# A recurrence fused with a feed-forward layer: shared table loads, one step's row sums on VectorE, another load order and new queue orders

## The chip, the cores and the metric

The kernel runs on one core of a Trainium2 chip. The metric is the device time of one execution in microseconds (us); the median of several runs counts. TensorE (PE) multiplies matrices, VectorE (DVE) and ScalarE (ACT) do elementwise work, ScalarE with function tables that it loads in sets, GpSimd (POOL) does a few memsets here, and SyncE (SP) issues most DMAs. TensorE's clock has two levels, 1.2 and 2.4 GHz; the profile shows the granted one as a share of the upper.

## What is computed

Shapes: 4 batches, 8 heads, 768 positions, head size 48; then 3072 tokens of width 384 and a hidden width of 2048. All in fp32.

```python
# recurrence, per batch and head
for t in range(S):
    kt, vt, rt = k[:, :, t], v[:, :, t], r[:, :, t]
    cur = einsum('bhd,bhe->bhde', u * kt, vt)
    y[:, :, t] = einsum('bhd,bhde->bhe', rt, state + cur)
    state = w * state + einsum('bhd,bhe->bhde', kt, vt)
# feed-forward
x = y.transpose(0, 2, 1, 3).reshape(3072, 384)
h = x @ w_in
g = h * tanh(softplus(h))
out = g @ w_out
```

## The kernel before

**Staging.** The 768 positions are cut into 6 chunks of 128. A *step* s is one chunk of one batch: 24 steps, s = 4 * chunk + batch. Four steps make the 512 tokens of a *group*; there are 6 groups. A step turns the recurrence into products: a matrix of scores (r against k, scaled by powers of w), masked, with a diagonal of row sums r*u*k (`dots`, `diag`), times v, plus the carried state times r; then the state is updated (`outputs`, `update_state`). For each group the feed-forward layer runs over 16 hidden tiles of 128: an *up* tile (x times w_in into a PSUM tile `hp`, of which there are two), evacuation to `hb`, the gate on ScalarE, and a *down* tile into three PSUM accumulators `acc`. Fp32 products are split into high and low parts with three passes, or done in the fp32 form in the first group, whose first eight up tiles are cut into halves so that steps 0 and 1 suffice to begin.

**Weights.** The 32 blocks of w_in and w_out (768 KB each) arrive as 64-bit words and are converted to fp32: one pass on ScalarE (L504) and three operations on VectorE (L508, L510, L514). Blocks are numbered in order of use: 0 to 3 are the first four of w_in, 4 is the first of w_out. Later they are split into high and low parts (L530, L532).

**Gates.** Two hidden tiles make a *batch* (48 in all, 8 per group). `act1`, `act2`, `act3` are sigmoid (L1094), arctan (L1097) and sine (L1100) over 128x1024 elements. Sigmoid and arctan share a table set, sine has another, so each batch has a table load at L1094 and one at L1100. Then `mix` multiplies (L1108, L1110) and splits (L1114, L1118) on VectorE. The `PAIRS` code, already there with an empty tuple, runs sigmoid and arctan for both batches of a pair before the two sines.

**Row sums.** Steps 0 and 1 form them as products on TensorE (`yt<-cst,q`). Steps 2 to N_PE - 1 form r*k on VectorE (L644) and sum it with one-column products on TensorE, merged with the scores (`pa<-cst,q`, 32 rows of the trace for each step). From step N_PE on VectorE does it all: two products (L686, L688) and a reduction (L691), from an `rkn` block that holds k and r and not k alone. `DIAG_ACT` names the steps whose diagonal ScalarE builds (L705, eight scalings); VectorE does the others in one operation (L707).

**Orders.** Every engine's instruction order is written out at build time by a planner (`Flow`): each piece of work is a thread with a rank, costs and named events, and a list of ranks and shifts (`RANK`, `CONVERT`, `SHIFT`, `LAG`, `AHEAD_*`, `DOWN`, `LO*`, `HI*`) sets which goes first. On the chip each engine then runs its queue in that order, with semaphores. `FIRST` is SP's order of the early loads, `REST` that of the later ones; weight blocks of `REST` go one at a time, and `GATE` lets block 3 and block 4 be issued only after TensorE has passed a certain product. An up tile needs a free `hp`, so it waits for the evacuation (`evacuate`, L1312) two tiles before; up tiles run at most 8 tiles ahead of down tiles.

**Idle products.** At the start TensorE multiplies zeros (128x512, bf16) where it would stand still. `WARM` says how many stand ahead of which product and which mark they wait for; `SHORT` adds short ones (128x16) ahead of step 0's row sums (14) and scores (28), and `LEFT_OUT` takes the long ones ahead of step 0's scores out.

Nearly all products are recorded at one line, L369, the helper `matmul`; the short idle products are at L399.

Of the kernel before, what the change touches and what calls it, by code (L numbers as in the profile page):

```python
# [62 lines left out]


N_DEC = 2
N_SQ, N_PE = 2, 6
OWN = 3
CHECK_AT, CHECK_STEP = 44, 3
DIAG_ACT = (0, 1, 2, 5, 6, 10)
AHEAD = 4  # L70
UNITS = [(h, c) for h in range(2) for c in range(AHEAD)] + [(None, f) for f in range(WG * AHEAD, NF)]

# [5 lines left out]
def first_use(c):  # L78
# [1 line left out]


FIRST = (
    ("rk", 0), ("rk", 1), ("raw", 0), ("rkn", 3), ("v", 0), ("rkn", 1), ("rk", 2), ("rkn", 2), ("raw", 1), ("v", 1),
    ("rkn", 0), ("v", 3), ("v", 2), ("rk", 3),
)
REST = (
    ("raw", 2), ("raw", 3), ("un", 0), ("raw", 4), ("rk", 4), ("v", 4), ("raw", 5), ("raw", 6), ("rkn", 4), ("raw",
    8), ("raw", 7), ("raw", 9), ("raw", 10), ("raw", 14), ("raw", 11), ("raw", 12), ("raw", 13), ("raw", 15),
)
LAND0, LAND = 3.15, dict(rk=1.32, v=0.66, raw=1.96, rkn=0.5, un=0.78)  # L90
ISSUE, QUEUED, LANDING, USE, BACKLOG = 0.5, 0.95, 1.9, 0.6, 4.2
GATE = dict(raw3=1, raw4=2)
HT = 2 * C
PAIRS = ()
BY_STEP = 0
FROM, FROM2 = 8, 14
X_SPLIT = 2
CONVERT = (1848.944, -4805.376, -1293.02, -2635.977)
LAG = 6
AHEAD_LEAST, AHEAD_MOST, DOWN = 3, 8, 0  # L100
LO0, HI0, LO1, HI1 = 0.0, 0.8, 0.05, 0.65
LAT, LAT0 = 0.15, 0.13
PE_GAP = 33
DVE_OWN = 0.02
COLD, COLD_END = 1.0, 0.0
WARM0, WARM_MIN, FILL = 10, 0.3, 0.28
WARM_END = 14.0
SHORT, LEFT_OUT = dict(dots0=14, attend0=28), ("attend0",)
WARM = dict(
    dots0=(("rk0", 2),), attend0=((None, 2),), dots1=((None, 1),), attend1=((None, 4),),  # L110
    outputs1=((None, 2), ("bent0", 3), ("whole0", 2), ("masked1", 4)),
# [2 lines left out]
BLOCK0, BLOCK, ASK, HELD, FETCH = 445, 256, 0.7, 2.9, 2.5  # L114
PATIENCE = dict(dve=0.1, act=0.1, pe=0.3)
URGENT = 8
RANK = dict(token_table=-1938.0, keys=833.2, first_state=-421.9)

COST = dict(dve=1.0)
FREE = dict(pe=5.6, act=2.8, dve=1.0, pool=1.7, sp=1.0, landed=1.0)  # L120
# [2 lines left out]


SHIFT = dict(
    attend10=98.0, attend5=51.0, convert11=-5.0, convert6=32.0, convert7=-243.0, convert9=122.0, diag10=-20.0,
    diag6=24.0, dots10=19.0, dots5=30.0, dots7=-71.0, dots8=121.0, evacuate10=-99.0, evacuate13=-164.0,
    evacuate22=-66.0, finish2=31.0, finish9=-62.0, gate10=141.0, gate12=-83.0, gate2=-42.0, gate3=54.0, gate8=-83.0,
    keys11=-152.0, keys5=24.0, mix0=-2.0, mix18=-54.0, mix5=-59.0, mix8=-31.0, mix9=-95.0, outputs9=-134.0,
    scale5=-174.0, split14=-67.0, split3=2.3, split4=73.0,  # L130
)


# [113 lines left out]
class Us(float):  # L247
    n = 0
# [17 lines left out]
def rwkv_mish_kernel(ctx, tc, rkT, rkN, vN, wT, w_in, w_out, consts, rkF, vF, wF, uF, outT):  # L266
    nc = tc.nc
# [9 lines left out]
    un = const.tile([128, DM], F32, name="un")  # L277
# [89 lines left out]
    def matmul(out, lhsT, rhs, **flags):  # L367
        nonlocal count
        ins = nc.tensor.matmul(out, lhsT=lhsT, rhs=rhs, **flags)  # L369
        first, count = count, count + (4 if lhsT.dtype == F32 else 2)  # L370
        k = (count - 1 - BLOCK0 % BLOCK) // BLOCK
        if k != (first - 1 - BLOCK0 % BLOCK) // BLOCK:
            crossed[k] = ins
        return ins
# [14 lines left out]
    def warm(name):  # L389

        z = zeros.bitcast(BF16)[:, :1]
        for after, n in WARM.get(name, ()):
            flow.begun += 2 * n
            for k in range(0 if name in LEFT_OUT else n):
                ins = matmul(idle, lhsT=z.broadcast_to([128, 128]), rhs=z.broadcast_to([128, 512]), start=True, stop=True)
                if after in marks and not k:
                    tc.add_manual_dep(ins.ins, marks[after].ins.name, sync, reason="no idle product goes too soon")
        for _ in range(SHORT.get(name, 0)):
            nc.tensor.matmul(  # L399
                idle[:32, :16], lhsT=z.broadcast_to([128, 32]), rhs=z.broadcast_to([128, 16]), start=True, stop=True  # L400
            )

    pa = ps.tile([128, 2, 512], F32, name="pa", tag="pa")
    for i in range(2):
# [5 lines left out]
    idle = ps.tile([128, 512], F32, name="idle", tag="acc0")  # L410
# [283 lines left out]
    def diag(s):  # L694
        yield f"sd{s}"
        if s >= 2:
            yield f"out{s - 2}"
        engine = yield {"act": 1.15} if s in DIAG_ACT else {"dve": 0.68}
        sd = sums.pop(s)
# [181 lines left out]
    def outputs(s):  # L881
# [33 lines left out]
        if not rows:  # L915
            flow.start(first_state(s), s + RANK["first_state"], name=f"first_state{s}")
        elif not last:
# [50 lines left out]
    def first_state(s):  # L968
        yield "out1"
        yield f"keys{s}"  # L970
        if s:
            yield f"state{s - 1}"
        yield pe(0.5, 64)
        state_products(s, new_first, True)
        for b in range(2):
            engine = yield {**act(192), **dve(192)}
            (nc.scalar.copy if engine == "act" else nc.vector.tensor_copy)(
                out=states[r112, 2 * s + b, :, :D], in_=new_first[b][r112]
            )
        flow.set(f"state{s}")  # L980
# [267 lines left out]
    def emitted(n, h):  # L1248
# [6 lines left out]
        if j == FB - 1:  # L1255
            two = b - 1 in PAIRS
            if b not in PAIRS:
                flow.start(gate(b - two, o, 1 + two), n - L_GATE, name=f"gate{b - two}")
# [62 lines left out]
    def gate(b, o, n=1):  # L1321
        t = act(o.n * o.T)["act"]
        for i in range(n):
            o = batches[b + i]
            for f in range(FB * (b + i), FB * (b + i + 1)):
                yield f"h{f}"
            if not b:
                yield "TKn"
            if b and not i:
                yield f"mixed{b - 1}"  # L1330
            if not i and b - 2 in PAIRS:
                yield f"mixed{b - 2}"
            yield {"act": t + 1.28 * (b > 0 and not i)}
            act1(o, second(b) if i else None)
            yield {"act": t}
            act2(o)
        if b == NC * NF // FB - 1:
            yield from last_gate(b, o)
            return
        for i in range(n):  # L1340
            yield {"act": t + 1.28 * (not i)}
            act3(batches[b + i])
            flow.start(mix(b + i), FB * (b + i + 1) - L_GATE, name=f"mix{b + i}")
# [122 lines left out]
    for s in range(NS):  # L1466
        if s < 2:
            flow.start(spread_v(s), rank(s) + 0.0045, 0.0, f"spread_v{s}")
        for k, thread in enumerate((load_step, load_v, scale, dots, diag, keys, attend, outputs)):
            if thread is keys and s >= NS - 2 or s <= B and thread in (load_step, load_v):  # L1470
                continue
            if thread is keys and s < B:
                flow.start(keys(s), s + (RANK["keys"] if s < 2 else -899.8), 0.0, f"keys{s}")
                continue
# [4 lines left out]
    for h in range(2) if FROM < WG * AHEAD else (None,):  # L1479
        flow.start(split_x(h), X_SPLIT, 0.0, f"split_x{'' if h is None else h}")  # L1480
    flow.start(load_rest(), -1200, 0.0)
    flow.start(prologue(), -1100, 0.0, "prologue")
    flow.start(token_table(), RANK["token_table"], 0.0, "token_table")
    for c in range(len(W_ORDER)):
        i, f = W_ORDER[c]
        at = first_use(f) + (LAG - L_OUT if i else -L_IN) + c / 1000
        flow.start(convert(c), CONVERT[c] if c < len(CONVERT) else at, 0.0, f"convert{c}")
    for n, (i, f) in enumerate(S_ORDER):
        first = first_use(f) if split_early((i, f)) else NF + f * WG
        flow.start(split(n), first + (LAG - L_OUT if i else -L_IN) + n / 1000, 0.0, f"split{n}")  # L1490
    flow.start(ups(), 1000, 0.0)
# [10 lines left out]
    with tc.If(in_range < 128 * N_FLAGS):  # L1502
# [3 lines left out]
        with tc.tile_pool(name="any1", bufs=1) as work:  # L1506
# [4 lines left out]
            z = work.tile([128, N, D], F32, name="z")  # L1511
# [39 lines left out]
        with tc.tile_pool(name="any2", bufs=1) as work:  # L1551
# [15 lines left out]
            z = zeros.bitcast(BF16)[:, :1]  # L1567
# [123 lines left out]
```

## Time and profile before

| what | value |
|---|---|
| median of 3 runs | 466.11 us (465.73 to 466.19) |
| the profiled execution | 465.52 us |
| its span, first to last instruction | 463.7 us |
| TensorE, ScalarE, VectorE busy | 98%, 86%, 80% of the span |
| mean granted clock of TensorE | 0.990 |

Busy shares are averages over stages: the start (about 20 us, until the first up tile), the first group with fp32 products (until about 110 us), and the rest. TensorE's ends are modelled, so a busy TensorE may still hide short waits; the waits view names those that show.

### The profile page before, as it was taken

Reading aid. Unit: us, or ns where it says so; the run is one execution under the profiler, and the core shown is the slowest. Engines: PE = TensorE matmul, PEld = TensorE weight load, DVE = VectorE, ACT = ScalarE, POOL = GpSimd, SP = SyncE. Lnnn points to the kernel's source line nnn. Section 1 sums busy time; section 2 is a strip of 40 time slices with the busy share of each in tenths; the row PEclk is TensorE's granted clock in tenths of the full one; section 3 lists DMA queues with packets and bytes.
Section 4 is the critical chain, followed back from the end, with each engine's and each line's share of the span. In section 5 each row is a group of like instructions: output and inputs, shape, how many; then the busy total and the mean of one; then the engine's idle time right before and its main releaser. Section 6 shows DMA issues by size and latency. Waiting matters only on the chain.

```text
span 463.7 us, 11622 instructions
## 1 busy us (share of the span) xinstructions
PE 454.9 (98%) x4966; PEld 385.4 (83%) x4966; DVE 368.9 (80%) x584; ACT 398.4 (86%) x515; POOL 4.4 (1%) x31
## 2 busy tenths in 40 slices
PE   8999999999999999999999999999999999999995
PEld 5688988756887888888888888888888888888884
DVE  6899999999799995699956789974898746646752
ACT  5678989999899897787899888899888899999981
POOL 1000000000000000000000000000000000000000
PEclk8899999999999999999999999999999999999999
DMA  8866765730422230334241545432353222142001
GB/s 294 324 221 212 278 220 174 259 107 1 166 87 84 69 103 9 121 131 144 90 154 54 191 158 201 157 112 69 146 174 109 75 80 69 68 136 70 1 1 72
DMA packets 20169, 60.16 MB, mean 130 GB/s; under 512 B 3312, under 2 KB 4304, under 8 KB 20112
## 3 DMA queue, kind: packets, MB, share of 16 engines
q1 hardware_dynamic: 17664, 55.11, 34.9%
q10 hardware_dynamic: 2448, 4.25, 2.4%
q8 instruction: 40, 0.66, 0.6%
q14 instruction: 17, 0.14, 0.1%
HBM read 52.57 MB, written 4.72 MB: 124 GB/s over the span
## 4 chain that ended last, share of the span: by engine, by line
PE 74%; ACT 11%; DVE 10%; issue 2%; DMA 1%; ACTq 1%; SPq 0%; DVEq 0%
PE hp L369 33%; PE acc L369 32%; PE pa L369 4%; DVE hb L1110 2%; PE yt L369 2%; ACT fa L1100 2%; ACT L1094 2%; ACT fa L1094 2%; ACT fa L1097 2%; ACT L1100 1%; PE idle L369 1%; DVE gl L1118 1%; DMA rk<-in_rkT_dram 1%; DVE w L532 1%; ACT we L451 1%
## 5 line engine op out<-in xcount | busy, mean ns | idle before, releaser
L369 PE MATMUL hp<-x,w 128*128 128x512 f32 x720 | 169.0, 381 | 0.9 <-DVE hb L1312 0.9
L369 PE MATMUL acc<-gh,w 128*128 128x512 f32 x492 | 158.2, 381 | 0.0
L369 PEld LDWEIGHTS hp<-x,w 128*128 128x128 f32 x720 | 135.2, 189 | 20.8 <-DVE hb L1312 1.1
L369 PEld LDWEIGHTS acc<-gh,w 128*128 128x128 f32 x492 | 93.0, 189 | 13.5
L369 PE MATMUL acc<-gl,w 128*128 128x512 f32 x246 | 92.6, 379 | 0.0
L1110 DVE TENSOR_TENSOR hb<-hb,fa 128x1024 f32<-128x1024 f32 x40 | 48.9, 1221 | 36.8 <-ACT fa L1100 36.6
L1094 ACT ACT_TABLE_LOAD x47 | 60.3, 1283 | 5.7 <-DVE hb L1110 4.6
L1100 ACT ACT_TABLE_LOAD x47 | 60.3, 1283 | 1.7 <-DVE rkn L686 0.9
L1094 ACT ACTIVATE fa<-hb,small 128x1024 f32<-128x1024 f32 x48 | 55.2, 1151 | 2.1 <-DVE hb L1110 1.5
L369 PEld LDWEIGHTS acc<-gl,w 128*128 128x128 f32 x246 | 46.5, 189 | 6.6
L1097 ACT ACTIVATE fa<-fa 128x1024 f32<-128x1024 f32 x48 | 50.7, 1057 | 1.1 <-ACT fa L1094 0.3
L1312 DVE COPY hb<-hp 128x512 f32<-128x512 f32 x48 | 32.7, 685 | 23.2 <-PE hp L369 22.9
L1100 ACT ACTIVATE fa<-fa 128x1024 f32<-128x1024 f32 x47 | 49.7, 1058 | 0.5
L1118 DVE TENSOR_TENSOR gl<-hb,gh 128x1024 fp32r<-128x1024 f32 x40 | 48.8, 1219 | 1.0 <-ACT gh L1114 0.4
L1312 ACT COPY hb<-hp 128x512 f32<-128x512 f32 x48 | 28.0, 583 | 18.8 <-PE hp L369 18.7
L369 PE MATMUL acc<-gf,wraw 128*128 128x256 f32 (+1 forms) x132 | 37.8, 439 | 0.8 <-PE hp L369 0.8
L369 PEld LDWEIGHTS acc<-gf,wraw 128*128 128x128 f32 x132 | 25.8, 196 | 10.6 <-issue 7.0
L640 DVE TENSOR_TENSOR rk<-rk,TR 112x1024 f32<-112x1024 f32 x22 | 26.7, 1216 | 0.1
L1114 DVE CAST gh<-hb 128x1024 fp32r<-128x1024 f32 x32 | 22.0, 687 | 1.1
L369 PE MATMUL hp<-x,wraw 128*128 128x256 f32 x96 | 22.5, 386 | 0.0
L369 PEld LDWEIGHTS hp<-x,wraw 128*128 128x128 f32 x96 | 18.4, 196 | 2.0
L451 ACT ACTIVATE we<-wraw 128x768 f32<-128x768 f32 x16 | 19.3, 1207 | 0.7 <-ACT we L1152 0.4
(150 smaller groups left out, 554.6 us busy)
## 6 DMA issues: line engine op xcount, KB each, us to landing
wraw<-in_w_in_dram SPq DMA_DIRECT2D x16, 768.0 KB, 4.2
wraw<-in_w_out_dram SPq DMA_DIRECT2D x16, 768.0 KB, 4.9
rk<-in_rkT_dram SPq DMA_DIRECT2D x22, 512.0 KB, 4.4
rkn<-in_rkN_dram SPq DMA_DIRECT2D x18, 384.0 KB, 4.5
v<-in_vN_dram SPq DMA_DIRECT2D x22, 256.0 KB, 4.6
out_dram<-ob ACTq DMA_DIRECT2D x10, 256.0 KB, 2.1
x<-x SPq DMA_DIRECT2D x60, 32.0 KB, 2.0
out_dram<-we ACTq DMA_DIRECT2D x6, 256.0 KB, 2.2
```

The source lines that it names most:

```text
L369: ins = nc.tensor.matmul(out, lhsT=lhsT, rhs=rhs, **flags)
L451: nc.scalar.activation(e, raw[:, :, 1].bitcast(F32), AF.Square, accum_out=to[:, 1:2])
L532: nc.vector.tensor_tensor(out=w[:, 1], in0=e, in1=w[:, 0].bitcast(F32), op=ALU.subtract)
L640: nc.vector.tensor_tensor(out=ab, in0=ab, in1=TR[:112].unsqueeze(1).broadcast_to([112, 4, NP, CK]), op=ALU.mult)
L1094: nc.scalar.activation(o.g, o.hb, AF.Sigmoid, bias=bias_ln2, scale=1.0)
L1097: nc.scalar.activation(o.g, o.g, AF.Arctan)
L1100: nc.scalar.activation(o.g, o.g, AF.Sin, scale=2.0)
L1110: nc.vector.tensor_tensor(out=o.hb, in0=o.hb, in1=o.g, op=ALU.mult)
L1114: (nc.scalar.copy if engine == "act" else nc.vector.tensor_copy)(out=o.gh, in_=o.hb)
L1118: nc.vector.tensor_tensor(out=o.gl, in0=o.hb, in1=o.gh.bitcast(F32), op=ALU.subtract)
L1312: (nc.scalar.copy if engine == "act" else nc.vector.tensor_copy)(out=to, in_=h)
```

## The change

Constants only, but for the short idle products, whose code goes. `N_PE` 5 makes step 5's row sums VectorE's. `DIAG_ACT` moves the diagonals of steps 2 and 10 to VectorE and that of step 8 to ScalarE. `PAIRS = (2, 19)` lets gate batches 2 and 3, and 19 and 20, share table loads. `FIRST` loads step 1's v fifth and not tenth, `REST` loads block 3 ahead of block 2. Without `SHORT` and `LEFT_OUT` the short idle products are gone, and the two long ones ahead of step 0's scores (`attend0` in `WARM`) are issued. The rest are ranks and limits of the planner.

```diff
-N_SQ, N_PE = 2, 6
+N_SQ, N_PE = 2, 5
-DIAG_ACT = (0, 1, 2, 5, 6, 10)
+DIAG_ACT = (0, 1, 5, 6, 8)
 FIRST = (
-    ("rk", 0), ("rk", 1), ("raw", 0), ("rkn", 3), ("v", 0), ("rkn", 1), ("rk", 2), ("rkn", 2), ("raw", 1), ("v", 1),
-    ("rkn", 0), ("v", 3), ("v", 2), ("rk", 3),
+    ("rk", 0), ("rk", 1), ("raw", 0), ("rkn", 1), ("v", 1), ("rkn", 3), ("v", 0), ("raw", 1), ("rk", 3), ("rk", 2),
+    ("v", 3), ("v", 2), ("rkn", 2), ("rkn", 0),
 )
 REST = (
-    ("raw", 2), ("raw", 3), ("un", 0), ("raw", 4), ("rk", 4), ("v", 4), ("raw", 5), ("raw", 6), ("rkn", 4), ("raw",
-    8), ("raw", 7), ("raw", 9), ("raw", 10), ("raw", 14), ("raw", 11), ("raw", 12), ("raw", 13), ("raw", 15),
+    ("raw", 3), ("raw", 2), ("raw", 4), ("raw", 5), ("un", 0), ("rk", 4), ("raw", 6), ("raw", 8), ("rkn", 4),
+    ("raw", 7), ("v", 4), ("raw", 10), ("raw", 14), ("raw", 9), ("raw", 11), ("raw", 12), ("raw", 15), ("raw", 13),
 )
-PAIRS = ()
+PAIRS = (2, 19)
-X_SPLIT = 2
-CONVERT = (1848.944, -4805.376, -1293.02, -2635.977)
-LAG = 6
-AHEAD_LEAST, AHEAD_MOST, DOWN = 3, 8, 0
-LO0, HI0, LO1, HI1 = 0.0, 0.8, 0.05, 0.65
+X_SPLIT = 3
+CONVERT = (2863.644, -4206.976, -1022.02, -2928.577)
+LAG = 8
+AHEAD_LEAST, AHEAD_MOST, DOWN = 1, 8, 2
+LO0, HI0, LO1, HI1 = 0.15, 0.95, 0.05, 0.9
-SHORT, LEFT_OUT = dict(dots0=14, attend0=28), ("attend0",)
-RANK = dict(token_table=-1938.0, keys=833.2, first_state=-421.9)
+RANK = dict(token_table=-1529.6, keys=1373.3, first_state=-698.4)
...
     def warm(name):
...
-            for k in range(0 if name in LEFT_OUT else n):
+            for k in range(n):
...
-        for _ in range(SHORT.get(name, 0)):
-            nc.tensor.matmul(
-                idle[:32, :16], lhsT=z.broadcast_to([128, 32]), rhs=z.broadcast_to([128, 16]), start=True, stop=True
-            )
```

`SHIFT`, a table of some 33 single shifts of rank (`evacuate13=-164.0` and the like), is replaced by another of the same size.

## Rows read from the trace of the kernel before

**Rows 1.** Page, busy time, share of the span and instructions of each engine.

```profile
PE 454.9 (98%) x4966; PEld 385.4 (83%) x4966; DVE 368.9 (80%) x584; ACT 398.4 (86%) x515; POOL 4.4 (1%) x31
```

**Rows 2.** Waits of TensorE: releaser, us in total, times, longest us.

```profile
PE hp L369 <- DVE hb L1312: 0.9, 1, 0.9
PE acc L369 <- PE hp L369: 0.8, 1, 0.8
...
PE pa L369 <- DVE rk L640: 0.6, 1, 0.6
```

**Rows 3.** Windows, 60 to 100 us: PE, PEld, DVE, ACT, POOL busy; PEclk; DMA share.

```profile
60.00:100.00 40.00, 40.00 (x524) 32.00 (x523) 39.97 (x67) 38.20 (x52) 0.31 (x4) 1.00 0.63 211
```

**Rows 4.** Chain that ended last, 0 to 60 us: start us, us, what.

```profile
6.15 0.44 PE idle L399 x14
...
7.57 0.83 PE idle L399 x28
8.40 1.06 PE pa L369 x32
...
10.01 1.50 PE yt L369 x8
11.51 1.73 PE idle L369 x4
...
15.10 2.51 PE idle L369 x11
```

**Rows 5.** Windows of 1 us where the granted clock, PEclk, falls and rises.

```profile
7.00:8.00 1.00, 1.00 (x25) 0.98 (x25) 1.00 (x2) 0.36 (x2) 0.00 (x0) 0.79 0.99 371
...
14.00:15.00 1.00, 1.00 (x60) 0.96 (x53) 0.58 (x2) 0.00 (x0) 0.00 (x0) 0.79 1.03 382
```

**Rows 6.** Chain that ended last, 20 to 60 us.

```profile
20.21 2.80 PE hp L369 x12
...
29.02 2.79 PE hp L369 x12
...
36.24 0.81 issue
37.05 2.84 PE acc L369 x12
39.88 1.09 PE pa L369 x64
...
49.31 1.40 PE pa L369 x95
```

**Rows 7.** Timeline of VectorE: start us, us, engine, line, operation, tiles.

```profile
35.99 0.95 DVE L514 CUSTOM_DVE_ANT_0 wraw<-wraw,we 128x1536 uint16<-128x1536 uint16 x1
```

**Rows 8.** Timeline of SP: start us, us, queue, line, operation, tiles.

```profile
18.79 0.33 SPq L488 DMA_DIRECT2D wraw<-in_w_in_dram  x1
```

**Rows 9.** DMA issues by line: count, KB each, median us to landing.

```profile
wraw<-in_w_in_dram SPq DMA_DIRECT2D x16, 768.0 KB, 4.2
```

**Rows 10.** Groups of VectorE by form: count | busy us, mean ns | idle before.

```profile
L686 DVE TENSOR_TENSOR rkn<-rkn,un 128x384 f32<-128x384 f32 x18 | 9.9, 548 | 0.0
...
L691 DVE TENSOR_REDUCE sd<-rkn 128x8 f32<-128x384 f32 x18 | 9.7, 544 | 0.2
...
L644 DVE TENSOR_TENSOR q<-rk 112x512 f32<-112x512 f32 x4 | 2.7, 685 | 1.0 <-DMA rk<-in_rkT_dram 1.0
```

**Rows 11.** Groups of ScalarE by form.

```profile
L1094 ACT ACT_TABLE_LOAD x47 | 60.3, 1283 | 5.7 <-DVE hb L1110 4.6 <-DVE gf L1108 0.3
L1094 ACT ACTIVATE fa<-hb,small 128x1024 f32<-128x1024 f32 x48 | 55.2, 1151 | 2.1 <-DVE hb L1110 1.5
L1097 ACT ACTIVATE fa<-fa 128x1024 f32<-128x1024 f32 x48 | 50.7, 1057 | 1.1 <-ACT fa L1094 0.3
```

**Rows 12.** Chain that ended last, 105 to 150 us.

```profile
148.55 0.60 DVE P L707
149.15 0.61 DVE hb L1312
```

More of the change, by code (lines that the diff above doesn't have):

```diff
@@ L125 @@
 SHIFT = dict(
[L126 to L130, printed above, removed]
+    attend4=47.0, attend9=-96.0, convert14=33.0, convert8=6.0, convert9=-118.0, dots1=-26.0, dots7=-127.0,
+    dots8=46.0, evacuate11=-4.0, evacuate30=-37.0, evacuate5=91.0, evacuate6=-25.0, gate1=15.0, gate14=-16.0,
+    gate19=81.0, gate2=27.0, gate7=-75.0, gate9=4.0, keys11=-0.3, keys7=-6.0, mix9=-63.0, outputs10=-151.0,
+    outputs11=-43.0, outputs13=56.0, outputs2=-19.0, outputs4=-130.0, outputs5=-185.0, outputs9=-93.0, scale12=27.0,
+    scale5=17.0, split0=24.0, split3=47.0, split9=-2.0,
 )
```

## The prediction

> **What bounds the kernel now.** I read the page first: TensorE is busy for 454.9 of 463.7 us, ScalarE for 86% and VectorE for 80% [rows 1]. A busy TensorE can hide waits, so the list of what TensorE waited for comes next: between the first tile and the last it names only three waits, 0.9, 0.8 and 0.6 us [rows 2]. Everything else there is products back to back. So no edit to VectorE or ScalarE can be worth more than the 2.3 us of these waits, except through the start, where TensorE's chain is idle products and small products strung on loads. That chain of waits is the third view [rows 4]; the stretches with the granted clock show that it runs partly at half speed [rows 5]. The fourth view is the chain from the first up tiles to the first down tile [rows 6], which ends at a VectorE conversion [rows 7]. VectorE is full in the stretch from 60 to 100 us (39.97 of 40.00) and ScalarE nearly (38.20) [rows 3], while TensorE there never waits: the two are just fast enough.
>
> **The change part by part.**
>
> *Short idle products.* The 14 short ones held the chain for 0.44 us and the 28 short ones for 0.83 [rows 4]: 1.27 us go. Two long idle products come in front of step 0's scores. One long product costs 0.43 us at the lower clock (1.73 over 4) or 0.23 at the upper (2.51 over 11) [rows 4], so 0.46 to 0.86 comes back. Net -0.81 to -0.41 on the chain of the start. The scores also need VectorE's product and scaling of step 0, which were done about when the short products ended, so I take -0.5. Whether it survives depends on the end of this stage: the first down tile at 37.05 waits 0.81 us [rows 6] for the third conversion operation on VectorE, which starts at 35.99 [rows 7]. If that one does not come earlier, nothing is gained: bounds 0 and -0.81.
>
> *Step 1's values sooner.* In the load order v1 moves from tenth to fifth; v0 goes from fifth to seventh and the rk block of step 2 from seventh to tenth. Step 1's outputs start behind eleven long idle products (2.51 us from 15.10) [rows 4], and those stay. So the earlier landing alone gives 0; it only keeps v1 from becoming the limit when the chain before it shortens. Step 2's rk comes later by three blocks of the list, but its products are not on TensorE before step 1's outputs are done; cost 0, with the cover of those idle products, and at most the 0.8 us by which the chain shortened if the cover fails.
>
> *Step 5's row sums on VectorE.* The sums were products on TensorE merged with the scores. A merged block with sums took 1.40 us, one without 1.09 [rows 6]: -0.31 on TensorE, which is the bound, so it counts in full. VectorE gives up one product of 0.685 and takes two products of 0.548 and a reduction of 0.544 [rows 10]: 0.685 out, 1.640 in, +0.96 us. The load of step 5's rkn block doubles. I take it as hidden behind step 4, which TensorE does first; bare, the 192 KB more cost about 1 us by the rate of [rows 9] (768 KB in 4.2 us). ScalarE loses one small copy.
>
> *Diagonals.* Steps 2 and 10 move from ScalarE to VectorE, step 8 the other way. VectorE's form holds the chain 0.60 us [rows 12], so VectorE gets +0.60 net. Together VectorE has 1.56 us more, almost all before 60 us. In the start it has gaps waiting for scores; in the full stretch [rows 3] it has none.
>
> *Two pairs.* Batches 2 and 3, and 19 and 20, do sigmoid and arctan for both, then sine for both. Each pair saves one load of each table, 1.283 us each [rows 11]: four loads, 5.13 us of ScalarE. None of it is TensorE time. What it can buy is part of the two later waits, 0.9 (an evacuation queued on VectorE behind other work [rows 12]) and 0.6 (a scaling on VectorE) [rows 2]. Both sit after long chains through ScalarE's gates, but each is in the end a matter of where an instruction stands in VectorE's queue, and all queues are reordered. Bounds 0 and -1.5; I take half, -0.75. The loads follow the work before them almost at once: the 47 before the sigmoid have 5.7 us of idle time together [rows 11], 0.12 each. The Trainium skill, page "ScalarE: Activation LUTs", section "What ACT_TABLE_LOAD costs", gives 1283 ns and a drain of about 1380 ns for each switch of tables; this trace agrees on the load and shows no such drain. By the page 10.6 us would come free, and I would take both waits as gone, 0.75 us below my sum.
>
> *Orders.* Ups go before downs on a tie (DOWN 2), downs may follow an up more closely, the recurrent steps are spread further along each group. TensorE's products are the same, so this is worth what waits it makes or takes. The 0.8 wait at 36.24 [rows 6] may shrink to nothing or stay: I keep it. Moving the fourth weight block ahead of the third costs something that is checked below. I take 0 for all of it, bounds -0.8 and +2.
>
> *Sum.* -0.5 - 0.31 - 0.75 = -1.56. The profiled execution took 465.52 us (span 463.7 and 1.8 around it), which gives 463.96; the median of the runs, 466.11, is 0.59 above it, so the prediction is 464.5 us. About 0.2%, 0.9 us, is what a measurement of this kernel can tell from no change.
>
> **The rivals.**
>
> *Absorbed: 465.8.* VectorE, with 1.56 us more, sets the first down tile where it was, and two new waits of the size of the old ones come up in the new order. Only the 0.31 of step 5 is left, 466.11 - 0.31. For it: the first down tile hangs on VectorE [rows 7] and VectorE has no gap in its full stretch [rows 3]. Against it: VectorE's gaps in the first 30 us, which a shorter chain of TensorE closes.
>
> *The third weight block is late: 467.3.* Block 3 is loaded before block 2 now, and its issue still waits for TensorE's instruction count: it went out at 18.79 [rows 8]. Both go one at a time. With 4.2 us from issue to landing [rows 9], block 3 would land at 22.5 (issued at 18.3, with the chain 0.5 shorter) and block 2 at 26.7. Its conversion needs about 1.9 us after that (ScalarE's pass and the last VectorE operation, both taken at the 0.95 of [rows 7]): 28.6. The third up tile, which reads block 2, started at 29.02 [rows 6], 28.5 after the shortening. So there is no slack: it decides once block 2 lands after about 26.7 or its conversion stands behind other work of VectorE, three operations of about 0.95 us at worst. That is +2.8 at this place, less the 1.56 of the sum: +1.2. Against it: with nothing else under way the landings could be quicker.
>
> *A pair starves the downs: 467.5.* The first batch of a pair waits for the second batch's up tiles (two at some 2.6 us, from 2.80 in [rows 6]) and its sigmoid and arctan (1.151 and 1.057) [rows 11], 7.4 us in all. Cover: ups that may run eight tiles ahead, and downs of earlier batches, about four tiles, some 8 us. If the lead is under three tiles, each pair costs the rest, 1.5 us a pair: +3.0 less 1.56.
>
> *The clock comes back sooner: 463.0.* The granted clock leaves the upper of its two levels (2.4 GHz) at 7.6 us for the lower (1.2) and is back at 14.4 (a mean of 0.79 between 1 and 0.5 is 0.58 of a microsecond at the upper) [rows 5], and this happens with the short products in place, after a stretch of idle time, short products and two-column products. Two long products now stand where 28 short ones stood. If this keeps or regains the upper level by about 10 us, the four idle products save 0.8 us (1.73 less 4 x 0.23) and the small products at 10.01, 1.50 us, up to half of theirs [rows 4]: -1.5 at most. The Trainium skill, page "TensorE: Matmul & The Clock Gate", section on the clock gate, says that activity of the array releases the throttle and that idling brings it back; by that rule the long products speak for this rival, and the gaps that the short ones filled speak against the change. No row here has the long ones in that place.
>
> **How the numbers follow.** Forecast 464.5 (its own range 463.4 to 465.2): 0.46. Clock: 0.11. Absorbed: 0.23. Third block: 0.12. Pairs: 0.08. Faster by over 0.2% is forecast and clock, 0.57; within 0.2% is absorbed, 0.23; slower is the other two, 0.20. The range 462.2 to 467.8 takes in the middle of every case; it leaves out the lower part of the clock case together with a complete loss of the waits, and the upper part of the two slow ones, under 0.2 together.
>
> **What would show it.** Right: step 0's scores start 0.4 us or more before 8.40; the first down tile starts before 36.7; the list of TensorE's waits sums to under 2.3 us after the first tile; four table loads fewer at unchanged 1.283 us; 32 fewer one-column products. Wrong: a wait for the third weight block's conversion near 28 us; a wait for gated values near a pair; an evacuation or scaling on VectorE late by over 1 us; the clock low past 14.4.

## The result, and the profile after

The changed kernel is slower: a median of 471.88 us (471.68 to 472.01) against 465.92 (465.57 to 466.19), ratio 1.0126 (1.0107 to 1.0144), so 5.96 us. The forecast was 464.5, the range 462.2 to 467.8. Line numbers behind the short idle products' code are 5 lower now (evacuation L1307, mask L761, conversion L499 to L509).

The profiled execution took 471.99 us, its span is 470.2. Busy times on the page (compare [rows 1]):

```profile
PE 456.7 (97%) x4897; PEld 384.3 (82%) x4897; DVE 370.6 (79%) x587; ACT 391.7 (83%) x499; POOL 4.5 (1%) x31
```

The work changed as the diff says: fewer products, ScalarE 6.7 us less busy, VectorE 1.7 us more. The planner also dealt the evacuations out anew, which the sums of the prediction do not have. VectorE does 54 of the 96 now (lines of the page, before and after):

```profile
L1312 DVE COPY hb<-hp 128x512 f32<-128x512 f32 x48 | 32.7, 685 | 23.2 <-PE hp L369 22.9
...
L1307 DVE COPY hb<-hp 128x512 f32<-128x512 f32 x54 | 37.2, 691 | 5.8 <-PE hp L368 5.8
```

None of that is a loss of 6.5 us of span. The list of TensorE's waits (as [rows 2]) shows where it is:

```profile
PE pa L368 <- DVE P L761: 2.2, 1, 2.2
PE hp L368 <- ACT hb L1307: 1.9, 2, 1.4
PE hp L368 <- DVE wraw L509: 1.2, 1, 1.2
PE yt L368 <- DVE P L761: 1.0, 1, 1.0
...
PE hp L368 <- DVE x L1011: 0.8, 1, 0.8
PE pa L368 <- DVE rk L635: 0.4, 1, 0.4
```

A mask (L761), an evacuation on ScalarE, the conversion of a weight block (L509) and a split (L1011) now end last. The chain of the start, where [rows 4] and [rows 6] stood:

```profile
12.83 2.51 PE idle L368 x11
...
17.77 2.80 PE hp L368 x12
...
22.02 2.80 PE hp L368 x12
...
26.48 0.05 PE hp L368
26.53 0.15 ACT sd L675
26.70 0.69 DVE P L702
27.39 0.47 DVE kn L714
27.86 0.64 DVE P L761
28.51 0.45 DVE we L503
28.98 0.97 DVE we L505
30.00 0.08 issue
30.08 0.97 DVE wraw L509
31.05 0.04 issue
31.09 5.49 PE hp L368 x12
...
38.27 2.79 PE hp L368 x12
41.07 5.18 PE acc L368 x24
```

The first up tile starts at 17.77, 2.44 us before that of [rows 6]. Then TensorE stands in the middle of step 2's outputs, from 26.48, for step 3's mask, and again until 31.09 for the conversion of block 2. The third up tile takes 5.49 us where an up tile takes 2.80. The first down tile starts at 40.9, on the chain at 41.07 (37.05 in [rows 6]). The windows say why the third up tile is slow (columns as in [rows 3]):

```profile
20.00:30.00 10.00, 7.74 (x303) 6.59 (x301) 9.37 (x15) 7.22 (x12) 0.09 (x1) 1.00 0.60 210
30.00:40.00 10.00, 8.91 (x116) 7.17 (x117) 6.72 (x13) 3.98 (x8) 0.09 (x1) 0.66 0.64 215
```

TensorE is busy for 7.74 of 10 us in the first (10.00 in the kernel before), and in the second the granted clock is 0.66 (1.00 before): 0.3 us into the second wait it went to the lower level, from 30.2 to 37.0. At the start it is the other way: the windows of [rows 5], 0.79 each there, are 1.00 and 1.00.

What else held block 2 up is in ScalarE's timeline, and in the view of the raw blocks' tile between 14 and 32 us (SP's issues: first and last start; then the landing):

```profile
25.46 1.15 ACT L1089 ACTIVATE fa<-hb,small 128x1024 f32<-128x1024 f32 x1
26.52 0.15 ACT L675 COPY sd<-pa 128x8 f32<-128x8 f32 x1
26.65 1.06 ACT L1092 ACTIVATE fa<-fa 128x1024 f32<-128x1024 f32 x1
27.61 0.89 ACT L499 ACTIVATE wraw<-wraw 128x768 f32<-128x768 uint32 x1
```

```profile
L483 SPq DMA_DIRECT2D wraw<-in_w_in_dram x2: 327/328/328, 17.8 to 22.4; - x2
...
DMA to landing us min/median/max: 4.2/4.5/4.6
```

Block 3 is issued at 17.8, block 2 at 22.4, when block 3 has landed. Block 2's landing is the quickest of the four in that view, 4.2 us, so it is there at 26.5. In the kernel before, block 2 went out ahead of the gate and landed at 20.7:

```profile
11.91 0.33 SPq L488 DMA_DIRECT2D wraw<-in_w_in_dram  x1
```

Now it stands behind block 3, which the gate holds as before. When it lands, ScalarE is in other work and the arctan until 27.6; VectorE has a diagonal, a key scaling and the mask ahead of its three operations, which take from 28.51 to 31.05 in the chain above.

Later the largest wait is at 166 us. ScalarE there:

```profile
163.38 1.28 ACT L1095 ACT_TABLE_LOAD   x1
164.67 1.06 ACT L1095 ACTIVATE fa<-fa 128x1024 f32<-128x1024 f32 x1
165.63 0.57 ACT L1307 COPY hb<-hp 128x512 f32<-128x512 f32 x1
```

The up tile that this evacuation empties had ended by 163.0; the evacuation stands behind a table load and a sine, and the next up tile, with a step's products between them, waits 1.4 us.

**The account** of this execution. Until the first down tile the changed kernel loses 3.9 us (2.4 won, 6.3 lost); of the 6.3, 3.35 are the two waits (2.16 and 1.19) and 2.7 the slow up tile. From the first down tile to the last accumulation it takes 424.5 us (40.9 to 465.4) where the kernel before takes 421.9: 2.6 us lost, in spite of step 5. The named waits there are 3.1 us against 1.5 [rows 2], so they cover 1.6 of the 2.6; the rest has no name in the profile. The second loss comes with the new orders whatever the start does: in this profile and in six of the experiments below that keep these orders and change at most the start, that stretch takes 424.0 to 425.7 us; in six with the old orders it takes 421.8 to 423.2. It is not independent of the start, though: 424.0 is the profile with the latest first down tile (42.8), and 425.7 that with the earliest (36.7).

### The profile page after: what moved, and what is told of

Same layout as the page of the kernel before. It is cut to its first block, busy times and chain, and to the rows that moved or that the text cites. A ratio compares the mean times of both kernels' runs of the same rounds, so it can differ in the third digit from the quotient of the medians.

```text
span 470.2 us, 11467 instructions
## 1 busy us (share of the span) xinstructions
PE 456.7 (97%) x4897; PEld 384.3 (82%) x4897; DVE 370.6 (79%) x587; ACT 391.7 (83%) x499; POOL 4.5 (1%) x31
## 4 chain that ended last, share of the span: by engine, by line
PE 61%; DVE 18%; ACT 16%; issue 2%; DMA 1%; SPq 1%; ACTq 0%; DVEq 0%
PE hp L368 29%; PE acc L368 26%; PE pa L368 3%; ACT fa L1095 2%; ACT L1089 2%; ACT L1095 2%; ACT fa L1089 2%; DVE w L527 2%; ACT fa L1092 2%; DVE rk L635 2%; DVE wraw L509 2%; DVE hb L1105 2%; DMA v<-in_vN_dram 1%; PE yt L368 1%; DVE we L505 1%
## 5 line engine op out<-in xcount | busy, mean ns | idle before, releaser
L368 PE MATMUL hp<-x,w 128*128 128x512 f32 x720 | 165.2, 382 | 2.3 <-ACT hb L1307 1.4
L368 PE MATMUL acc<-gh,w 128*128 128x512 f32 x492 | 153.4, 380 | 0.0
L1105 DVE TENSOR_TENSOR hb<-hb,fa 128x1024 f32<-128x1024 f32 x39 | 47.7, 1222 | 45.5 <-ACT fa L1095 45.3
L1089 ACT ACT_TABLE_LOAD x45 | 57.7, 1283 | 12.1 <-DVE hb L1105 8.2
L1089 ACT ACTIVATE fa<-hb,small 128x1024 f32<-128x1024 f32 x46 | 52.9, 1151 | 0.7 <-DVE hb L1105 0.2
L1092 ACT ACTIVATE fa<-fa 128x1024 f32<-128x1024 f32 x46 | 48.7, 1058 | 0.8
L1095 ACT ACTIVATE fa<-fa 128x1024 f32<-128x1024 f32 x45 | 47.6, 1058 | 0.5
L1307 DVE COPY hb<-hp 128x512 f32<-128x512 f32 x54 | 37.2, 691 | 5.8 <-PE hp L368 5.8
L1307 ACT COPY hb<-hp 128x512 f32<-128x512 f32 x42 | 24.4, 581 | 18.9 <-PE hp L368 18.9
L368 PEld LDWEIGHTS acc<-gf,wraw 128*128 128x128 f32 x132 | 25.7, 196 | 9.0 <-issue 7.0
L368 PE MATMUL hp<-x,wraw 128*128 128x256 f32 x96 | 24.7, 417 | 1.2 <-DVE wraw L509 1.2
L368 PEld LDWEIGHTS hp<-x,wraw 128*128 128x128 f32 x96 | 20.0, 213 | 4.0 <-DVE wraw L509 1.3
L1109 DVE CAST gh<-hb 128x1024 fp32r<-128x1024 f32 x28 | 19.3, 689 | 3.4 <-PE acc L368 2.2
```

Source lines behind the costliest of these rows:

```text
L1089: nc.scalar.activation(o.g, o.hb, AF.Sigmoid, bias=bias_ln2, scale=1.0)
L1092: nc.scalar.activation(o.g, o.g, AF.Arctan)
L1095: nc.scalar.activation(o.g, o.g, AF.Sin, scale=2.0)
L1105: nc.vector.tensor_tensor(out=o.hb, in0=o.hb, in1=o.g, op=ALU.mult)
```

## The experiments

Each profile is one execution, and executions of one kernel spread, some by 4 to 6 us, so times below are medians, and places are from the profile. The kernel before was run beside each set: 466.3, 466.1, 466.1, 466.3 and 466.2 us.

**Short idle products out of the old kernel, and back into the new one.**

```diff
-SHORT, LEFT_OUT = dict(dots0=14, attend0=28), ("attend0",)
```

> The kernel before without its 42 short idle products and with the two long ones ahead of step 0's scores; its queue orders stay. If the short products let the clock fall at the start, it now stays at the upper level past 8 us, the first up tile starts 1.5 to 2.5 us sooner than 20.2, and the total falls by 0 to 1.5 us, as far as VectorE's conversions let the first down tile follow. Rival: the new load order kept the clock up in the changed kernel; then the clock falls here as before, the first up tile starts at 19.7 or later and the total falls by 0.5 at most.

Measured: 466.32 (464.73 to 468.47), ratio 1.0007 (0.9984 to 1.0029). In the profile the clock does not fall at the start, and first up and first down tile come 1.0 and 0.8 us earlier, but TensorE stands still for 1.73 us in the row sums of step 2, with no releaser named.

> The changed kernel with the 42 short idle products put back in place of the two long ones, orders unchanged. If they let the clock fall: lower level from about 7.6 to 14 us, first up tile 1.5 to 2.5 us later than 17.7. The total rises by less than that, 0 to 1 us, because the third up tile waits for its weight block anyway. Rival (load order): the clock stays up and the total moves by under 0.3.

Measured (the line and its code put back into the changed kernel): 473.46, ratio 1.0138 (1.0096 to 1.018). The clock is low from 7.8 to 14.7 again and the first up tile starts at 19.8. So with the short products in place of the two long ones the clock falls (whether the short ones or the missing long ones do it, these runs do not separate), and without them the start is about 2 us shorter under the new orders; under the old ones nothing of it reaches the median.

**Blocks 2 and 3 exchanged, all orders kept** (block 2 is loaded and converted where the change has block 3).

```diff
+    SWAP = {2: 3, 3: 2}
...
-        ins = nc.sync.dma_start(raws[c], weights(c))
+        ins = nc.sync.dma_start(raws[SWAP.get(c, c)], weights(SWAP.get(c, c)))
...
-        raw = raws[c]
+        raw = raws[SWAP.get(c, c)]
...
-        whole[W_ORDER[c]] = up.bitcast(F32)
+        whole[W_ORDER[SWAP.get(c, c)]] = up.bitcast(F32)
```

> The changed kernel with blocks 2 and 3 exchanged in their loads and conversions, every queue's order as it was: the third up tile's block is then converted at 26.3 and not 31.0. If the late block and the clock that falls behind it are the main loss: the wait of 1.2 us ahead of the third up tile goes, the clock stays up if the remaining 2.2 us of idle time does not bring it down, and the total falls by 4 us (1.2 and 2.8), or by 1.2 if the clock falls all the same. Rival (later orders are the main loss): the total falls by under 1 us, what is won is given back at the waits after 60 us.

Measured: 471.14, ratio 1.0108 (1.0089 to 1.0127). The wait ahead of the third up tile is gone and the clock stays up at 30 us, but the wait for the mask stays (2.2 us), and the first down tile is at 38.6. In this profile the clock was low earlier, from 11.7 to 15.1, and the first up tile started at 19.1; from there to the first down tile it takes 19.5 us, the changed kernel 23.2. The median is 0.5 to 0.7 us below the changed kernel's two (471.88 and, in the repeat below, 471.59), which their spread takes in. The same exchange in the old kernel, which puts block 3 first there:

> The kernel before without the short idle products, with blocks 2 and 3 exchanged in loads and conversions (block 3 is loaded first, as in the change) and every order otherwise as it was. Rival of the prediction (third block late decides): the third up tile, 28.14 in the kernel without short products, starts 1.4 to 2.8 us later with a named wait for a conversion, and up to 2.8 us more if the clock falls there: 467.7 to 471.9. Forecast of the prediction (no slack needed, orders worth nothing): 28.1 and 466.3 as before.

Measured: 467.75 (465.61 to 468.49), ratio 1.0025 (1.001 to 1.004); the third up tile waits 1.2 us and starts at 31.24, against 28.14 in the profile without the exchange; 1.9 us of that difference were there at the second up tile already, since the clock was low from 19.7 to 23.1 and the first up tile took 1.7 us longer. For the wait the profile names a copy of x there, which had ended by 30.7; the last operation of block 2's conversion runs from 30.20 to 31.14, so that is what it waited for. It is a milder exchange than the change's: the gate stays with the second transfer, so block 2 lands at 23.3 and not at 26.5, and is late because its last operation has block 3's place in VectorE's queue. Against the two medians without the exchange (466.32, 466.67) it costs 1.1 to 1.4 us, part of which goes with the clock: the three executions at a mean granted clock of 0.999 or 1.000 took 465.6 to 466.7 us, the seven at 0.994 to 0.996 467.4 to 468.5.

**Long idle products in the two gaps.**

```diff
+        if s == 2:
+            idle_products(9)
         carried(0)
...
         hp = hp_tile(f"h{n}")
+        if n == 2:
+            idle_products(5)
```

> The changed kernel with 9 long idle products in the wait inside step 2's outputs and 5 in the wait ahead of the third up tile. They fill 3.0 of the 3.4 us, so both waits stay. If the clock's fall at 30.6 is a cost of its own, the third up tile takes 2.8 and not 5.5 us and the total falls by 2.5 to 3 us. Rival (only the waits cost, what follows has slack): under 0.5 us.

Measured: 470.25, ratio 1.0089 (1.0056 to 1.0122). The granted clock is 1.00 until the end, the third up tile takes 2.7 us instead of 5.49, and the first down tile comes 3.0 us earlier. The waits are what they were; the products only fill them. The same window in the changed kernel and here, and the third up tile here:

```profile
26.00:32.00 6.00, 2.65 (x122) 2.31 (x112) 5.74 (x12) 5.97 (x9) 0.09 (x1) 0.85 0.59 184
...
26.00:32.00 6.00, 5.59 (x125) 3.62 (x116) 5.74 (x12) 5.86 (x9) 0.09 (x1) 1.00 0.55 184
...
31.15 2.67 PE hp L368 x12
```

So the fall of the clock is a cost of its own: the last accumulation ends 2.4 us earlier in the profile. The median is 1.3 to 1.6 lower than the changed kernel's two, which the spread of the repeat (469.33 to 475.23) takes in.

**The mask behind the outputs, alone and with the exchange.**

```diff
         yield f"diag{s}"
+        if s == 3:
+            yield "out2"
         yield dve(560)
```

> The changed kernel as it is, on the chip of the next three, as their reference: 471 to 472.5 us, and the same waits of TensorE after 60 us as in its first profile if these come from the order and not from chance.

Measured (the changed kernel again, as reference): 471.59 (469.33 to 475.23); the same waits, and one of 0.7 us for an evacuation on VectorE at 85 us.

> The changed kernel with step 3's masking put behind step 2's outputs in the plan, as it was before; the order of the start is otherwise kept, that of later stages may shift. If the 2.2 us wait inside step 2's outputs is the masking's place in VectorE's queue: that wait goes, and the third up tile still waits for block 2. If block 2's conversion is then the limit, it comes sooner by up to 1 us only (its load lands at about 27) and the total falls by under 1 us plus what the clock gives back (2.8 if it stays up). Rival (the wait was the limit of all that follows): the total falls by 2.2 to 5 us.

Measured: 471.06, ratio 1.0098 (1.0072 to 1.0125). The wait in step 2's outputs shrinks from 2.2 to 1.3 us, the third up tile starts at 31.2 as before: the mask alone was not the limit, block 2 is.

> Both: step 3's masking behind step 2's outputs, and blocks 2 and 3 exchanged. If the two waits and the clock that falls in them are the loss of the start: no wait over 0.5 us between 20 and 36, no low clock there, first down tile at 35 to 37, total 5 to 6.5 us below the changed kernel. Rival (later waits are a loss of their own): first down tile as said, but the total falls by only 2 to 4.5 us, with waits of some 2.5 us left after 60 us.

Measured: 470.16, ratio 1.0096 (1.0071 to 1.012). Third up tile at 28.6, first down tile at 36.7, 0.4 us ahead of [rows 6], no low clock. The start is repaired, and 4 us of the loss are still there (470.16 against 466.06). In the profile 4.3 us are won until the first down tile and 1.2 given back behind it (425.7 for 424.5); the median is only 1.4 to 1.7 below the changed kernel's two.

**One sine behind one evacuation,** on top of both. TensorE's order is the same.

```diff
         for i in range(n):
+            if b == 12:
+                yield "h28"
             yield {"act": t + 1.28 * (not i)}
             act3(batches[b + i])
```

> The changed kernel with the two earlier repairs (mask of step 3 behind the outputs of step 2, blocks 2 and 3 exchanged) and one more: the sine of gate batch 12 goes behind the evacuation of tile 28 in ScalarE's queue. TensorE's order stays as it is, and the other engines' orders up to that place. Theory (the later loss is a few instructions that stand at the wrong place of a queue, each wait counts in full): the wait of about 1.6 us near 161 goes, 1.3 to 1.6 us less span from first down tile to last accumulation, median about 468.7. Rival (the later loss is work that VectorE and ScalarE do not get done in time): the wait comes back at the next tiles, median 470.2 as without it.

Measured: 469.17, ratio 1.0071 (1.0045 to 1.0096). The wait near 161 is gone (ScalarE's evacuations hold TensorE up for 0.5 us in all, before for 1.9) and the span is 1.1 us shorter; a wait of 1.1 us for VectorE's evacuation at 81 us, 0.7 in the repeat and absent in the first profile, shows here. The four executions (467.80 to 470.44) overlap those without the move (468.88 to 471.44), so the medians alone do not show the gain. One such move in the old kernel (step 11's diagonal behind tile 25's evacuation):

```diff
+        if s == 11:
+            yield "h25"
         engine = yield {"act": 1.15} if s in DIAG_ACT else {"dve": 0.68}
```

> The kernel before without the short idle products, with the diagonal of step 11 moved on VectorE from ahead of the evacuation of tile 25 to behind it; TensorE's order is the same. Theory (a wait of TensorE counts in full, whatever engine it comes from): the wait of 1.0 us near 148 goes down to 0.3 or less, 0.7 to 1.0 us less than the same kernel without the move. Rival (the next instruction of that queue is late in its place): no change within 0.3 us, with a new wait within some 10 us behind it.

> The kernel before without the short idle products once more, as the reference: 466.3 median, in a spread of 464.7 to 468.5; the wait of 1.0 us near 148 is there.

Measured: 466.24 (465.03 to 468.12) against 466.67 (465.17 to 468.05). The wait for the evacuation went from 1.0 to 0.4 us, and one of 0.2 came up 5 us behind it. Between theory and rival; the difference is within the spread.

**One constant at a time.** These four have the planner make all orders anew, with the shifts of the kernel that they start from.

```diff
-LO0, HI0, LO1, HI1 = 0.0, 0.8, 0.05, 0.65
+LO0, HI0, LO1, HI1 = 0.15, 0.95, 0.05, 0.9
```

> The kernel before without the short idle products, with the changed kernel's four limits that spread the recurrent steps along a group (LO, HI) and nothing else: no work is added or taken away on any engine. Theory (an order made with shifts that were not made for it costs 1 to 3 us by itself): 467.5 to 469.5, in new waits of 0.5 to 1.6 us for evacuations, scalings and splits. Rival (orders are worth nothing, as the prediction has it): 466.3.

Measured: 478.75, ratio 1.0295 (1.0249 to 1.0342), 12.1 to 12.4 us more than the two medians without it, with no work added anywhere. TensorE's waits in that kernel:

```profile
PE acc L368 <- DVE gh L1109: 2.3, 1, 2.3
PE acc L368 <- ACT gh L1109: 2.1, 1, 2.1
PE acc L368 <- DVE gl L1113: 1.8, 3, 0.9
```

> The kernel before without the short idle products, with the two pairs and nothing else; the orders are made again around them with the old shifts. Prediction's step: up to 1.5 us less, half of it likely, from the two later waits: 465.6. Theory (TensorE waits on none of the 5.1 us of ScalarE that come free): no gain, what shows is the new orders, 466 to 468.5 with a wait or two that the kernel without pairs does not have. Rival (the first batch of a pair starves the downs): 1.5 us a pair, 469.3, with a wait of an accumulation for gated values at tiles 4 to 7 and near tile 38.

Measured (`PAIRS = (2, 19)`): 476.75, ratio 1.0251 (1.0197 to 1.0305). The rival's wait is there, at one pair, and larger than priced:

```profile
PE acc L368 <- DVE gf L1103: 4.7, 1, 4.7
```

> The kernel before without the short idle products, with step 5's row sums on VectorE (N_PE 5) and nothing else; orders made again with the old shifts. Theory: TensorE loses 32 one-column products, 0.31 us; the orders cost what they cost, so 466.0 less or more one wait. Rival (VectorE's 0.96 us are not hidden between 30 and 60 us): 466.9 to 467.3, with TensorE waiting for a mask or a conversion before step 5.

Measured (`N_PE` 5): 476.37, ratio 1.0213 (1.0196 to 1.023), with waits for states, scalings and splits of weights.

> The changed kernel with step 5's row sums back on TensorE. By the price of the prediction +0.3 us on TensorE and 0.96 less on VectorE near 60 us. If VectorE's extra work made the waits after 60 us, they shrink and the total falls by 0.5 to 2; if not, it rises by 0.3 or moves by what the replanned order happens to give, under 1 either way.

Measured (`N_PE` 6 in the changed kernel): 486.07, ratio 1.0417 (1.039 to 1.0444). So each of the four orders made anew with another kernel's shifts loses 10 to 14 us, whichever constant moves. That the shifts are the reason is not shown: in the first of them the new limits may be the worse ones by themselves. These four say nothing of the parts' own prices, and both theories on them fell.

**The saved table loads put back, all orders kept.** A sine of one column between the batches of each pair forces the two tables in again.

```diff
+            if i:
+                spare = const.tile([128, 1], F32, name=f"spare{b}")
+                nc.scalar.activation(spare, bias_ln2, AF.Sin)
             act1(o, second(b) if i else None)
```

> The changed kernel with one sine of one column put between the two batches of each pair, so that the two tables are loaded once more for each pair (four loads, 5.1 us of ScalarE, are back) while all orders stay as they are. If the saved loads are worth nothing to TensorE: the same as the changed kernel, 471.7 within 0.5. Prediction's step: 0.75 to 1.5 us slower, 472.5 to 473.3. Rival (the pairs need the time, their downs are close behind): 1.5 us or more a pair, 474.5, with waits for gated values or evacuations near 50 to 70 and near 200 us.

Measured: 476.72 (476.45 to 476.79), ratio 1.0228 (1.0208 to 1.0248): 4.8 us more than the changed kernel, the four loads being 5.1 and the two added sines 0.2 each. In the profile the clock is also low from 72.1 to 75.5, which it is not in the changed kernel, so part of the 4.8 may be the clock's. ScalarE and VectorE of that kernel at the first pair:

```profile
62.68 1.28 ACT L1331 ACT_TABLE_LOAD   x1
63.97 0.20 ACT L1331 ACTIVATE spare<-small 128x1 f32<-128x1 f32 x1
64.18 1.28 ACT L1089 ACT_TABLE_LOAD   x1
65.48 1.15 ACT L1089 ACTIVATE ga<-hb,small 128x1024 f32<-128x1024 f32 x1
66.53 0.24 ACT L1008 CAST x<-yt 128x128 fp32r<-128x128 f32 x1
```

```profile
66.81 0.29 DVE L1011 TENSOR_TENSOR x<-yt,x 128x128 fp32r<-128x128 f32 x1 [2.76 <-ACT x L1008]
67.02 1.09 DVE L505 SCALAR_TENSOR_TENSOR we<-wraw,we 128x768 uint32<-128x768 uint32 x1
68.04 0.42 DVE L1011 TENSOR_TENSOR x<-pa,x 128x256 fp32r<-128x256 f32 x1
68.37 0.95 DVE L509 CUSTOM_DVE_ANT_0 wraw<-wraw,we 128x1536 uint16<-128x1536 uint16 x1
69.23 0.69 DVE L1307 COPY hb<-hp 128x512 f32<-128x512 f32 x1
```

The late sigmoid delays a small copy of x on ScalarE, VectorE idles 2.76 us for it, and behind it in VectorE's queue stands the evacuation that empties the `hp` tile which a step's products need next. VectorE's evacuations cost TensorE 4.2 us in three waits there (1.9 at 70 us, 2.1 at 241, behind the second pair, and 0.2), none of them in the changed kernel's list (0.7 in its repeat).

**Five long idle products in the stall of the old kernel's start.**

```diff
             warm(f"attend{s}")
+            if s == 2:
+                z = zeros.bitcast(BF16)[:, :1]
+                for _ in range(5):
...
             scores(s)
```

> The kernel before without the short idle products, with five long idle products ahead of step 2's row sums, where that kernel stood still for 1.73 us with no releaser named; all orders as they were. If the stall ends at a fixed moment (something that arrives, not something that TensorE asks for when it gets there): the products fill it, the first up tile stays near 19.1, the clock stays up more often and the median goes from 466.3 to about 464.9. Rival (the stall follows the products): the first up tile at 20.2, 467.4.

Measured: 466.43 (464.59 to 468.23), ratio 1.0006 (0.999 to 1.0022). The stall without a releaser is gone from the profile and the first up tile is at 20.0, of which a late v block explains 0.6: the stall mostly had a fixed end. But the median did not move, and executions at a mean granted clock of 1.00 took from 464.6 to 468.2 us. My idea that the clock makes the spread fell.

No version beats the kernel before by more than can be told.

## Why the prediction was wrong

**The step that failed** is "Orders": "I take 0 for all of it, bounds -0.8 and +2". TensorE's products are the same, as it says, but the term is what waits the orders make, and I bounded it by the waits that the old trace shows plus one place. The runs show other bounds: moving three of the planner's four limits alone cost 12 us, and each of the four kernels with orders made anew lost 10 to 14. The new orders came with shifts of their own and lost less: 3.9 us until the first down tile and 2.6 behind it in the profile. Of the 2.6, 1.6 are named waits, which I read as single instructions behind others in a queue; one, the evacuation behind a sine, went when the sine was moved. The rest has no name.

**The third block.** That step let the load order go at nothing. The rival with the price for it held: it put block 2's landing at 26.7 (measured 26.5) and the third up tile at +2.8 (it started at 31.09, 2.6 us after the 28.5 that the sum needed). Its own sum, 28.6 and so just in time, had one term mis-sized: 1.9 us from the landing to the whole block, for ScalarE's pass and the last VectorE operation. The other two VectorE operations read the landed block too. Block 1 in the kernel before, which landed at 15.0:

```profile
15.59 0.92 ACT L504 ACTIVATE wraw<-wraw 128x768 f32<-128x768 uint32 x1
...
16.22 0.55 DVE L508 TENSOR_SCALAR we<-wraw 128x768 uint32<-128x768 uint32 x1
16.81 0.96 DVE L510 SCALAR_TENSOR_TENSOR we<-wraw,we 128x768 uint32<-128x768 uint32 x1
17.91 0.96 DVE L514 CUSTOM_DVE_ANT_0 wraw<-wraw,we 128x1536 uint16<-128x1536 uint16 x1
```

It was whole 3.8 us behind its landing, block 0 as well, and block 2 5.0 (20.7 to 25.7). With 3.8 the rival's sum comes to 30.5, 2.0 us late: it was the case to expect, and not one of 0.12. In the changed kernel it became 4.5 us, with the arctan ahead of it on ScalarE and diagonal, key scaling and mask on VectorE. What the rival lacked besides was the next link: in the second of the two waits the clock fell, and the next up tile took another 2.7 us. The idle products in the gaps and the exchange of the blocks each show one link; the mask, which I first took for the limit, was only beside it.

**Short idle products.** I took -0.5. Step 0's scores started 0.8 us earlier and the clock did not fall at 7.6, which I had as a rival of 0.11; together the first up tile came 2.44 us earlier. The Trainium skill, page "TensorE: Matmul & The Clock Gate", section "What's actually happening", has activity release the throttle; the trace agrees as far as long products go (1.00 with them, 0.79 with the short ones in their place, in the windows of [rows 5]). The gain ended at the next limit, block 2, with step 3's mask beside it; the text expected the limit at another conversion, that of the first down tile's block.

**Pairs.** -0.75 was the term, up to -1.5. Under the new orders putting the four loads back costs 4.8 us, since they do not only lengthen two old waits: they make copies and evacuations behind them late, and in the profile the clock falls once more. Whether orders made without pairs would do without them was not tried. The rival of starved downs did not come in the changed kernel, but did in the old orders (4.7 us at one pair).

**Step 5, diagonals, values.** There are 32 one-column products fewer (96 for 128) and two table loads fewer at each of the two lines, at 1.283 us as before. VectorE's extra work did not show as a wait by itself. Step 1's values cost and brought nothing that shows; step 0's, which went back to make room, land at 10.9 (10.1 before) and now stand on the chain of the start, but VectorE was in a conversion until then anyway. The term of -0.31 rests on a misreading of [rows 6]: the block of 1.09 at 39.88 holds step 4's 32 sums and 32 scores, and that of 1.40 at 49.31 step 5's sums and scores and 31 more products. In the kernel before, step 5's sums start at 49.14 and its scores at 49.58, so the sums hold the scores up by 0.44 us. What that is worth to the total could not be measured alone.

**Open.** With the start repaired and one sine moved, 3.0 us of the loss remain (469.17 against 466.13). The profile shows waits of 0.2 to 1.1 us, at a mask, a state, an evacuation, a split, a scaling; I did not take them away one by one, and from the first down tile on they are only part of the loss. What spreads the executions of one kernel over 4 us is open too.

## What to carry to other kernels

When a change replaces every queue's order, the old trace cannot price the order: set its bounds from kernels whose orders were made anew, not from the waits that the old order left. Follow each transfer that is issued one at a time through to its first reader, with the instructions that stand ahead of each step of its conversion in their queues, and price that conversion by what the old trace took from landing to use, not by a choice of its operations. A wait of TensorE of some us near the start has a second price, the clock behind it, and work taken off an engine that is no bound can still be worth nearly all of its time where small copies queue behind it.

## What was not expected of the hardware

- Short products (128x16, bf16) keep TensorE busy in the records, yet the clock fell to its lower level at 7.6 to 7.8 us in the profiles of both kernels that have them; in the 17 profiles without them it fell near there once (7.3), though in seven it fell somewhere in the first 23 us. It does not fall in every execution: of 73 of the kernel before beside these runs, 4 had a mean granted clock of 0.998 or more, where 6.8 us at the lower level alone would make 0.993.
- In the second of two waits (2.16 and 1.19 us, with small products between them) the clock fell and was low for 6.8 us; with nine and five long idle products put into the same gaps it never fell.
- TensorE stood still for 1.1 to 1.7 us amid 32 equal one-column products, with nothing named, in the seven profiles with the old load order and neither short products nor idle ones ahead of that place; idle products there took up most of that time. In all seven a 16 KB transfer of an instruction queue starts 2.4 to 2.6 us before the stall ends; the changed kernel has such a transfer at 14.5 us and no stall there, so it is not shown to be the cause.
